# Any free PSUM bank, named in a written order, in place of a ring of six and a ring of two

## The chip, the cores and the metric

The kernel runs on one core of one Trainium2 chip. The metric is the device time of one execution in microseconds (us), as the median of several runs. One further execution was recorded by the hardware profiler; its rows are what the reader sees below. Engines are named as in the profile: PE is the matrix engine, PEld its weight loads, DVE, ACT and POOL the vector, scalar and general engines, SP the engine that issues stores and transposing DMAs.

## The reference, cut to what matters

```python
# q, k, v: (4, 8, 768, 64) float32;  w_in: (512, 2048);  w_out: (2048, 512);  result (3072, 512) float32
scores = q @ k^T / 8 - slope[h] * dist          # per batch and head
keep   = (column < 8) | (0 <= row - column < 96)   # 8 global keys and a window of 96
a      = softmax(where(keep, scores, -1e9))
x      = (a @ v) as (3072 tokens, 512)
out    = relu(x @ w_in) ** 2 @ w_out
```

## The kernel before, in words

The 3072 tokens are 24 tiles of 128 (six a batch), and each two tiles make a block of 256 tokens, 12 blocks in all. Every piece of work is an *op* with a name, made by `Plan.op`. The names that matter here, with the line that the profile shows for their instructions:

- `ld.q.j`, `ld.k.j`, `ld.v.j`, `ld.win.s.c`, `ld.wout.s` (L267): loads of the first tiles and of all weights, one DMA each, issued by POOL. `load.j` (L270), for tiles 6 and up, issues three of them: q, k and v of tile j. All these loads are on one queue and convert float32 to bf16. A ring of eight semaphores makes POOL wait, before each load, for the landing of the eighth load before it.
- `tr`, `T` (L463, L390/L392): transposes of q and k of tiles 0 to 5 on PE, and the copies out of PSUM. From tile 6 on, `T.j` (L487) is one transposing DMA that SP issues. SP issues in its own order, and the instruction waits only for what it reads, for its buffer, and for a semaphore of its own ring.
- `bias`, `sc` (L530, L550): the scores of a tile, in groups of eight matmuls that use half the rows of the PE array each; two PSUM banks a group. `exp` (ACT, L616), `mul` (DVE, L641), `pv` (PE, L703), `norm` (DVE, L733/L734) follow.
- `trx`, `xT` (L771, L390/L392): the attention result transposed, on PE for tiles 0 to 7, later by a transposing DMA (L795).
- `s1.b.s` (PE, L826): step s of eight of the first matrix product of block b, eight matmuls of 128x256 into one bank. `relu` (ACT, L849) and `sq` (ACT L865 or DVE L867) follow.
- `s2.0.s.sub` (PE, L1104): the second product of block 0, with `w_out` as it is. For blocks 1 to 11 the second product is made as seven smaller ones, `s2.b.p1` to `p7`, each in two halves `.0` and `.1` (PE, L975, four matmuls of 128x256 a half). They need sums of the squares (`sum`, DVE) and of the weights (`wsum`, DVE); `p1` and `p2` read `w_out` itself: half `.1` of them reads pieces 4 to 7, the fourth matmul piece 7. `part` and `o` evacuate, `st` (SP) stores.
- `gate.j` (DVE, L436): a tiny write to the buffer that `load.j` fills, so that this load waits for DVE.

No scheduler runs on the chip or in the build. The string `ORDER` lists every op once, in the order in which the program emits them; `@A` and `@V` choose ACT or DVE. Each engine then works through its own instructions in that order, and waits on semaphores for the others.

PSUM has eight banks. Before, they are two pools: `ps_g` with six buffers under one tag, `ps_acc` with two. A new user of a pool gets the buffer after the last one given, round and round, and waits for that buffer's last reader. `ps_acc` holds the first tiles' `pv` and the second product's sums; all else takes turns in `ps_g`:

```python
ps_acc = ctx.enter_context(tc.tile_pool(name="ps_acc", bufs=NACC, space=PSUM))   # NACC = 2
ps_g = ctx.enter_context(tc.tile_pool(name="ps_g", bufs=NG, space=PSUM))         # NG = 6
...
tiles["hT", blk, s] = ps_g.tile([P, 2, 2 * P], FP32, name="hT", tag="g")
...
pool, tag = (ps_g, "g") if last else (ps_acc, "acc")
tiles["acc", blk, bank] = pool.tile([P, HN], FP32, name="acc", tag=tag)
```

Of the kernel before, what the change touches and what calls it, by code (L numbers as in the profile page):

```python
# [59 lines left out]
exp.3.1.0 s1.0.0#2 s1.0.0#3 s1.0.0#4 ld.win.3.0 s1.0.6 norm.2.1 mul.3.0.0 gv.2 ld.k.4 mul.3.1.0 trx.2 mul.3.0.1  # L60
exp.3.1.1 ld.q.4 mul.3.1.1 pv.3.0 pv.3.1 norm.3.0 norm.3.1 relu.0.0 xT.2@A relu.0.6 ld.win.4.0 s1.0.3 s1.0.3#2 gk.3
sq.0.0@A ones.6 trx.3 tr.1.4 T.1.4@A relu.0.3 ld.win.1.0 tr.0.4 xT.3@V sq.0.6@A s1.1.0 T.0.4@V s1.1.6 ld.q.5 ld.k.5
relu.1.0 s1.1.4 sq.0.3@V sq.1.0@V relu.1.6 ld.win.2.1 ld.win.2.0 gv.3 s1.0.1 sq.1.6@V relu.1.4 s1.0.1#2 sc.4.0
sq.1.4@A relu.0.1 tr.0.5 ld.wout.0 exp.4.0.0 s1.1.3 sq.0.1@V sc.4.1 T.0.5@A s1.0.4 mul.4.0.0 exp.4.1.0 ld.win.5.0 E0.1
ld.v.4 s1.0.2 relu.1.3 sq.1.3@A exp.4.1.1 gk.4 s1.1.2 ld.win.7.0 mul.4.1.0 s2.0.0.0 tr.1.5 relu.1.2 s2.0.0.1 exp.4.0.1
s1.0.2#2 s1.0.2#3 sq.1.2@V ld.v.5 T.1.5@A mul.4.0.1 s1.0.2#4 relu.0.4 ld.wout.2 s1.0.5 ld.wout.1 relu.0.2 sq.0.4@V
pv.4.0 s1.1.7 sq.0.2@A mul.4.1.1 norm.4.0 relu.0.5 relu.1.7 pv.4.1 sc.5.0 norm.4.1 sc.5.1 ld.wout.5 exp.5.0.0 sq.0.5@V
s1.1.5 sq.1.7@A gv.4 mul.5.0.0 exp.5.1.0 exp.5.1.1 s1.0.7 exp.5.0.1 ld.wout.3 relu.1.5 mul.5.1.0 trx.4 xT.4@V
mul.5.0.1 s2.0.1.0 mul.5.1.1 pv.5.0 ld.wout.4 norm.5.0 relu.0.7 s1.1.1 ld.wout.7 pv.5.1 norm.5.1 s2.0.1.1 s2.0.2.1
# [5 lines left out]
exp.6.0.0 sq.2.4@V wsum.3.1 s2.1.p5.1 exp.6.1.0 sc.7.0 mul.6.0.0 sc.7.1 s2.1.p7.0 exp.7.0.0 T.8 s2.1.p7.1 gate.9
sq.2.2@A mul.6.1.0 exp.7.1.1 part.1.p7@V s1.2.1 exp.7.1.0 mul.7.0.0 pv.6.0 mul.7.1.1 o.1.p5 exp.7.0.1 norm.6.0 pv.6.1
relu.2.1 mul.7.1.0 mul.7.0.1 s2.1.p4.0 s2.1.p4.1 sq.2.1@A o.1.p4@A s2.1.p3.0 s2.1.p3.1 norm.6.1 load.9 st.1.1 pv.7.1
pv.7.0 o.1.p3 s2.2.p1.0 st.1.0 norm.7.0 trx.6 norm.7.1 s2.2.p1.1 s2.2.p2.0 xT.6@A trx.7 T.9 gk.7 sum.2.0 s2.2.p2.1
xT.7@V sc.8.0 sc.8.1 s1.3.0 s1.3.3 gate.10 sum.2.1 exp.8.0.0 exp.8.1.0 s1.3.7 part.2.p1@A relu.3.0 load.10 exp.8.0.1
gv.7 mul.8.0.0 sum.2.2 sq.3.0@A s1.3.2 exp.8.1.1 mul.8.0.1 s2.2.p6.0 mul.8.1.0 relu.3.7 s2.2.p6.1 relu.3.2 mul.8.1.1  # L80
load.11 sq.3.7@V o.2.p2 pv.8.1 pv.8.0 relu.3.3 s1.3.5 part.2.p6@A norm.8.0 s2.2.p5.0 s2.2.p7.0 sq.3.3@A sq.3.2@A gk.8
sum.2.3 relu.3.5 s2.2.p5.1 sc.9.0 norm.8.1 gv.8 xT.8 exp.9.1.0 mul.9.1.0 sc.9.1 T.10 load.12 sq.3.5@V exp.9.0.0
exp.9.1.1 mul.9.0.0 exp.9.0.1 s2.2.p7.1 s1.3.1 part.2.p7@V mul.9.1.1 s1.3.6 o.2.p5 relu.3.1 relu.3.6 s1.3.4 sq.3.1@A
pv.9.0 mul.9.0.1 s2.2.p4.0 norm.9.0 pv.9.1 norm.9.1 gk.9 s2.2.p4.1 relu.3.4 sq.3.4@A o.2.p4@A s2.2.p3.0 s2.2.p3.1
sq.3.6@A xT.9 s2.3.p1.0 load.13 o.2.p3 s2.3.p1.1 sum.3.0 s2.3.p2.0 part.3.p1@A T.11 sum.3.1 s2.3.p2.1 sum.3.2 sc.10.0
exp.10.1.0 sc.10.1 s2.3.p6.0 s2.3.p6.1 o.3.p2 exp.10.0.0 gv.9 mul.10.1.0 s2.3.p5.0 s2.3.p5.1 part.3.p6@V exp.10.0.1
mul.10.0.0 exp.10.1.1 s2.3.p7.0 mul.10.0.1 load.14 gk.10 mul.10.1.1 s2.3.p7.1 part.3.p7@A pv.10.0 pv.10.1 s1.4.0
norm.10.0 s1.4.7 norm.10.1 relu.4.0 sc.11.0 sc.11.1 s1.4.4 T.12 relu.4.7 s1.4.3 sq.4.0@V exp.11.0.0 o.3.p5 exp.11.1.1
gv.10 mul.11.0.0 exp.11.1.0 s1.4.2 sq.4.7@V exp.11.0.1 load.15 mul.11.1.0 pv.11.0 relu.4.4 mul.11.1.1 mul.11.0.1
relu.4.3 sc.12.0 sq.4.4@A sq.4.3@V s1.4.5 xT.10 st.2.0 relu.4.2 norm.11.0 exp.12.1.0 pv.11.1 s1.4.6 relu.4.5  # L90
exp.12.0.0 s1.4.1 sq.4.2@V mul.12.1.0 sq.4.5@A s2.3.p4.0 norm.11.1 mul.12.0.0 s2.3.p4.1 pv.12.0 xT.11 relu.4.6
relu.4.1 sum.3.3 sq.4.6@A sq.4.1@V T.13 s2.3.p3.0 o.3.p4@A st.2.1 sum.4.0 s2.3.p3.1 o.3.p3 pv.12.1 sum.4.1 sum.4.2
s2.4.p1.0 s2.4.p1.1 s2.4.p2.0 s2.4.p2.1 part.4.p1@A s2.4.p6.0 s2.4.p6.1 part.4.p6@A o.4.p2 s2.4.p5.0 s2.4.p5.1
s2.4.p7.0 s2.4.p7.1 norm.12.0 norm.12.1 load.16 sc.13.0 sc.13.1 s1.5.0 exp.13.1.0 xT.12 T.14 mul.13.1.0 exp.13.1.1
T.15 exp.13.0.0 sum.4.3 s1.5.3 relu.5.0 part.4.p7@A s1.5.5 mul.13.0.0 mul.13.1.1 exp.13.0.1 sq.5.0@V s2.4.p4.0 pv.13.0
s1.5.1 mul.13.0.1 pv.13.1 relu.5.5 sq.5.5@V s1.5.6 relu.5.3 relu.5.1 norm.13.0 norm.13.1 sq.5.1@A xT.13 sq.5.3@V
s1.5.2 s2.4.p4.1 s1.5.4 relu.5.6 o.4.p5 s1.5.7 s2.4.p3.0 s2.4.p3.1 relu.5.2 sq.5.6@A o.4.p4@V st.3.1 gv.13 gk.13
load.18 sq.5.2@V relu.5.4 relu.5.7 sq.5.4@V sc.14.0 sq.5.7@A o.4.p3 sc.14.1 exp.14.0.0 s2.5.p1.0 s2.5.p1.1 s2.5.p2.0
s2.5.p2.1 sum.5.0 exp.14.1.0 st.3.0 T.16 load.17 part.5.p1@A sum.5.1 exp.14.1.1 mul.14.0.0 mul.14.1.0 mul.14.1.1
s2.5.p6.0 s2.5.p6.1 sum.5.2 pv.14.0 exp.14.0.1 s1.6.1 s1.6.0 norm.14.0 part.5.p6@A kl.14 relu.6.0 mul.14.0.1 o.5.p2  # L100
kl.15 relu.6.1 s2.5.p7.0 pv.14.1 s2.5.p7.1 norm.14.1 sq.6.0@A s2.5.p5.0 part.5.p7@A xT.14 sc.15.0 sc.15.1 s2.5.p5.1
s1.6.4 s1.6.3 exp.15.0.0 sum.5.3 exp.15.1.0 s2.5.p4.0 mul.15.0.0 exp.15.0.1 gv.14 sq.6.1@V s1.6.2 s2.5.p4.1 exp.15.1.1
mul.15.0.1 mul.15.1.1 relu.6.3 mul.15.1.0 o.5.p5 st.4.0 load.19 sq.6.3@A relu.6.4 pv.15.0 s2.5.p3.0 norm.15.0 relu.6.2
pv.15.1 o.5.p4@A norm.15.1 sc.16.1 sq.6.2@V sc.16.0 xT.15 s1.6.7 s2.5.p3.1 sq.6.4@A exp.16.1.0 exp.16.0.0 mul.16.1.0
# [1092 lines left out]
```

## Time and profile before

| | us |
|---|---|
| median of 3 runs | 204.45 (204.17 to 205.06) |
| span of the profiled execution, first to last instruction | 202.7 |
| what lies outside the span, median less span | 1.75 |
| PE busy | 196.9 (97%) |
| DVE, ACT, POOL busy | 148.4, 146.1, 75.4 |
| software DMA queue (the loads of POOL), share of 16 engines | 89.0% |

A row of the profile's timeline gives the start and the duration of one or several merged instructions, their engine, line and tiles, and in brackets how long the engine was idle before and what ended that. Matmuls are pipelined: a 128x256 one has a duration of about 270 ns, but the next starts 109 ns later, so work is counted here by the distance of starts. The landing of a DMA is the moment when its semaphore has reached its full count; the profile's DMA view gives the time from issue to landing.

### The profile page before, as it was taken

How to read it: one execution, taken by the hardware profiler on the slowest of the kernel's cores; microseconds unless marked ns; L12 is line 12 of the kernel's file. 1: busy time of each engine (PE TensorE's matmuls, PEld its weight loads, DVE VectorE, ACT ScalarE, POOL GpSimd, SP SyncE). 2: the span in 40 equal slices, each digit the busy share in tenths (PEclk: the TensorE clock that was granted, in tenths of full speed). 3: DMA queues.
4: the chain of work that ended last, by engine and by line, in shares of the span. 5: the costliest groups of instructions: out<-in, count | busy, mean ns of one | idle time of the engine just before them, and what ended most of it. 6: DMA issues, size and time to landing. Idle time of an engine off the chain costs nothing.

```text
span 202.7 us, 5686 instructions
## 1 busy us (share of the span) xinstructions
PE 196.9 (97%) x2272; PEld 166.7 (82%) x2272; DVE 148.4 (73%) x404; ACT 146.1 (72%) x289; POOL 75.4 (37%) x93
## 2 busy tenths in 40 slices
PE   7899999999999999999999999999999999999993
PEld 3668878678889888888988988989988888988883
DVE  8289567882897777885888679679669887717843
ACT  6778899448959865964886987696597677848520
POOL 8999776623339425705059004550130000000000
PEclk9999999999999999999999999999999999999999
DMA  8999999999599999996999956999595323031022
GB/s 126 153 173 179 180 184 205 192 147 182 136 175 139 155 130 121 193 179 91 118 235 137 160 118 145 129 160 204 107 143 105 100 78 29 12 118 55 0 110 102
DMA packets 113965, 27.38 MB, mean 135 GB/s; under 512 B 105490, under 2 KB 111122, under 8 KB 113938
## 3 DMA queue, kind: packets, MB, share of 16 engines
q0 software_dynamic: 80256, 13.37, 89.0%
q1 hardware_dynamic: 33682, 13.64, 33.4%
q8 instruction: 18, 0.29, 0.6%
q14 instruction: 9, 0.07, 0.1%
HBM read 27.26 MB, written 6.29 MB: 166 GB/s over the span
## 4 chain that ended last, share of the span: by engine, by line
PE 88%; POOL 6%; DMA 3%; DVE 0%; issue 0%; POOLq 0%
PE hT L826 41%; PE acc L975 34%; PE sc L550 5%; PE po L703 5%; PE acc L1104 3%; DMA qk<-in_q_dram 3%; POOL qk L267 3%; POOL v L267 2%; POOL win L267 1%; PE tr L463 0%; PE trx L771 0%; DVE o L1051 0%; POOL pbi L327 0%; POOLq L327 0%; POOLq L1178 0%
## 5 line engine op out<-in xcount | busy, mean ns | idle before, releaser
L826 PE MATMUL hT<-xT,win 128*128 128x256 bf16 (+1 forms) x800 | 93.8, 268 | 0.0
L826 PEld LDWEIGHTS <-win 128*128 128x128 bf16 x800 | 74.0, 98 | 9.8
L849 ACT ACTIVATE hr<-hT 128x512 f32<-128x512 f32 x96 | 56.0, 605 | 20.8 <-PE hT L826 17.4
L616 ACT ACTIVATE esc<-sc 128x512 bf16<-128x512 f32 x78 | 42.5, 606 | 5.9 <-PE sc L550 5.3
L270 POOL DMA_DIRECT2D qk<-in_q_dram x18 | 16.2, 902 | 66.9 <-DMA qkT<-qk 51.3
L867 DVE TENSOR_TENSOR hs<-hr 128x512 bf16<-128x512 f32 x43 | 29.5, 685 | 15.7 <-ACT hr L849 15.5
L975 PEld LDWEIGHTS <-hsum 128*128 128x128 bf16 x360 | 33.5, 98 | 5.0 <-issue 0.6
L641 DVE TENSOR_TENSOR at<-esc,E 128x512 bf16<-128x512 bf16 x78 | 30.6, 417 | 6.7 <-ACT esc L616 6.3
L975 PE MATMUL acc<-wsum,hsum 128*128 128x256 bf16 x264 | 34.3, 273 | 0.0
L865 ACT ACTIVATE hs<-hr 128x512 bf16<-128x512 f32 x53 | 33.2, 634 | 0.7
L975 PEld LDWEIGHTS <-hs 128*128 128x128 bf16 x264 | 25.0, 98 | 2.9
L975 PE MATMUL acc<-wout,hs 128*128 128x256 bf16 x176 | 23.0, 273 | 0.0
L1051 DVE TENSOR_TENSOR o<-acc,part 128x256 f32<-128x256 f32 (+2 forms) x34 | 14.0, 411 | 10.7 <-PE acc L975 9.3
L734 DVE TENSOR_TENSOR x<-po,rs 128x256 bf16<-128x256 f32 x48 | 20.4, 424 | 1.7
L390 ACT COPY part<-acc 128x256 f32<-128x256 f32 x24 | 9.0, 374 | 15.0 <-PE acc L975 14.6
L703 PE MATMUL po<-v,at 128*128 128x65 bf16 x352 | 17.8, 194 | 0.4 <-DVE v L751 0.3
L703 PEld LDWEIGHTS <-at 128*128 128x128 bf16 x352 | 15.8, 98 | 2.2 <-issue 0.4
L270 POOL DMA_DIRECT2D v<-in_v_dram x18 | 16.4, 911 | 1.3 <-DMA wout<-in_moe_w_out_dram 1.3
L270 POOL DMA_DIRECT2D qk<-in_k_dram x18 | 16.2, 898 | 0.6 <-DMA wout<-in_moe_w_out_dram 0.6
L932 DVE TENSOR_TENSOR hsum<-hs 128x1024 bf16<-128x1024 bf16 (+1 forms) x24 | 15.4, 641 | 1.3 <-ACT hs L865 1.0
L733 DVE RECIPROCAL rs<-po 128x4 f32<-128x4 f32 x48 | 8.6, 179 | 8.7 <-PE po L703 8.2
L550 PEld LDWEIGHTS <-qkT 64*128 64x128 bf16 x312 | 9.5, 94 | 4.6 <-issue 4.0
(62 smaller groups left out, 182.2 us busy)
## 6 DMA issues: line engine op xcount, KB each, us to landing
out_dram<-o SPq DMA_DIRECT2D x22, 256.0 KB, 2.6
v<-in_v_dram POOLq DMA_DIRECT2D x24, 128.0 KB, 5.6
qk<-in_k_dram POOLq DMA_DIRECT2D x23, 128.0 KB, 5.4
qk<-in_q_dram POOLq DMA_DIRECT2D x23, 128.0 KB, 4.8
wout<-in_moe_w_out_dram POOLq DMA_DIRECT2D x8, 256.0 KB, 9.2
win<-in_moe_w_in_dram POOLq DMA_DIRECT2D x6, 256.0 KB, 7.3
win<-in_moe_w_in_dram POOLq DMA_DIRECT2D x4, 128.0 KB, 6.3
out_dram<-o SPq DMA_DIRECT2D x3, 128.0 KB, 1.7
```

The lines of the kernel that those rows point to most:

```text
L270: nc.gpsimd.dma_start(out=dst, in_=src)
L550: nc.tensor.matmul(out=tiles["sc", j, odd, g][:, at, :], lhsT=left[j - 1][half, pair, :] if kt else qkT[j % NKT][half, 1, pair, :], rhs=qk ...
L616: nc.scalar.activation(out=esc, in_=tiles.pop(("sc", j, odd, g)).rearrange("p a c -> p (a c)"), func=Act.Exp, scale=scale,)
L641: nc.vector.tensor_mul(at, tiles.pop(("esc", j, odd, g)), bias)
L703: nc.tensor.matmul(out=po[:, hi, :], lhsT=tiles["at", j, odd, g][:, at * P : (at + 1) * P], rhs=v_sb[kj][:, h, :], start=(i == 0), stop=(i ...
L734: nc.vector.tensor_tensor(out=x[:, 4 * hf : 4 * hf + 4, :], in0=po[:, :, :D], in1=rs.to_broadcast([P, 4, D]), op=Alu.mult,)
L826: nc.tensor.matmul(out=hT[:, c, cols], lhsT=w_in_sb[s][:, kt, c * P : (c + 1) * P], rhs=tiles["xT", blk][:, kt, cols], start=(kt == 0), st ...
L849: nc.scalar.activation(hr, tiles.pop(("hT", blk, s)), Act.Relu)
L865: nc.scalar.activation(hs, hr, Act.Square)
L867: nc.vector.tensor_mul(hs, hr, hr)
L932: nc.vector.tensor_tensor(out=t[:, i, h], in0=t[:, a, h] if isinstance(a, int) else half_a(blk, *a)[:, h], in1=t[:, b, h] if isinstance(b, ...
L975: nc.tensor.matmul(out=tiles["acc", blk, bank][:, cols], lhsT=left_[:, s], rhs=right_[:, cols], start=first and s == 0, stop=s == NSTEP - ...
```

## The change

All eight banks become eight tiles of their own, made once. A word of `ORDER` can end in a colon and one digit for each bank that the op opens: `sc.7.1:13` takes banks 1 and 3, `s1.2.2:6` takes bank 6. `run` keeps the digits in `o["banks"]`, and `psum(n)` hands the n-th of them to the op. Round-robin is gone; a user still waits for the last reader of its bank. The warm-up matmuls write bank 7. The amount and the kinds of work are the same: the same ops are emitted, with the same shapes. The order of all of them, and the choice of ACT or DVE for some copies and squares, is another. Of the new order these stretches are shown: the loads near the start, `load.6`, `load.7` and `load.8` among the pieces of `w_out`, the first use of pieces 0 to 7, and the end.

```diff
-    def run(self, free=()):
+    def run(self):
...
         for word in ORDER.split():
+            word, _, banks = word.partition(":")
             name, _, letter = word.partition("@")
...
+            o["banks"] = [int(b) for b in banks]
...
-s1.0.2#2 s1.0.2#3 sq.1.2@V ld.v.5 T.1.5@A mul.4.0.1 s1.0.2#4 relu.0.4 ld.wout.2 s1.0.5 ld.wout.1 relu.0.2 sq.0.4@V
...
-s2.0.2.0 s2.0.3.0 sq.1.5@V trx.5 s2.0.4.0 s2.0.5.0 s2.0.3.1 s2.0.4.1 wsum.0.0 relu.1.1 ld.wout.6 load.6 load.7 xT.5@V
...
-s1.2.5 load.8 s2.1.p1.1 sum.1.3 part.1.p1@A s1.2.4 wsum.1.1 relu.2.5 o.0.1@A s2.1.p6.0 relu.2.7 s1.2.2 st.0.1 sq.2.5@A
...
-o.11.p4@V st.11.1#2 s2.11.p3.0 s2.11.p3.1 o.11.p3 st.11.0#2 s2.11.p3.0#2 s2.11.p3.1#2 o.11.p3#2 st.11.0#3
...
+pv.5.0:7 norm.5.0 load.6 load.7 s1.1.5:1 norm.5.1 relu.1.1 s1.1.2:0 ld.wout.0 trx.5:7 ld.wout.2 sq.0.5@V sq.1.1@A
+ld.wout.1 s1.1.4:3 xT.5@V s1.2.0:2 E0.1 relu.1.2 sq.1.2@A s1.2.5:6 s1.2.6:4 T.6 ld.wout.3 relu.0.2 s2.0.0.1:7 relu.2.0
+sq.0.2@V sq.2.0@V relu.2.5 s2.0.0.0:0 T.7 s1.2.7:5 s1.2.4:2 gate.8 relu.1.5 sq.2.5@V s2.0.1.0 s1.2.3:6 sq.1.5@V
+ld.wout.4 relu.1.4 sq.1.4@V sum.1.0 s2.0.2.0 s2.0.1.1 s2.0.2.1 relu.2.7 load.8 T.8 sq.2.7@V sc.7.1:13 wsum.2.0
+relu.2.6 relu.2.4 wsum.0.0 sum.1.2 sc.7.0:54 sq.2.6@A sum.1.1 relu.2.3 ld.wout.5 sc.6.0:26 gk.7 sq.2.4@V exp.7.1.1
+ld.wout.6 exp.6.0.0 exp.7.0.1 sum.1.3 s2.0.3.1 s2.0.3.0 ld.wout.7 mul.7.1.1 s2.1.p2.0:3 mul.6.0.0 exp.6.1.0 s2.0.4.1
+s2.0.4.0 mul.7.0.1 s2.1.p1.0:2 wsum.1.0 exp.7.1.0 s2.0.5.0 s2.0.5.1 mul.6.1.0 pv.6.0:1 gate.9 exp.7.0.0 mul.7.1.0
+s1.2.2:6 pv.6.1:4 mul.7.0.0 norm.6.0 s2.0.6.0 norm.6.1 wsum.0.1 s2.1.p1.1 relu.2.2 pv.7.0:5 sq.2.3@A load.9 trx.6:1
...
+st.11.1#2 s2.11.p3.0 s2.11.p3.1 o.11.p3 st.11.0#2 s2.11.p3.0#2 s2.11.p3.1#2 o.11.p3#2 sum.10.3 part.10.p1@A s2.10.p6.0
+s2.10.p6.1 s2.10.p2.0:5 s2.10.p2.1 part.10.p6@A s2.10.p7.0 s2.10.p7.1 o.10.p2 s2.10.p5.0 s2.10.p5.1 part.10.p7@V
+s2.10.p4.0 s2.10.p4.1 o.10.p5 st.11.0#3 s2.10.p3.0 o.10.p4@A st.10.1 s2.10.p3.1 o.10.p3 st.10.0
...
-    NG = 8 - NACC
-    G = ("g", NG)
+    NBANK = 8
+    G = ("bank", NBANK)
...
-    ps_acc = ctx.enter_context(tc.tile_pool(name="ps_acc", bufs=NACC, space=PSUM))
-    ps_g = ctx.enter_context(tc.tile_pool(name="ps_g", bufs=NG, space=PSUM))
+    ps = ctx.enter_context(tc.tile_pool(name="ps", bufs=1, space=PSUM))
...
+    banks = [ps.tile([P, 4 * P], FP32, name=f"bank_{i}", tag=f"bank_{i}") for i in range(NBANK)]
+    given = []
+
+    def psum(n=0, dt=FP32):
+        b = banks[given[n]]
+        return b if dt == FP32 else b.bitcast(dt)[:, : 4 * P]
...
-                tiles["hT", blk, s] = ps_g.tile([P, 2, 2 * P], FP32, name="hT", tag="g")
+                tiles["hT", blk, s] = psum().rearrange("p (a c) -> p a c", a=2)
...
-                            pool, tag = (ps_g, "g") if last else (ps_acc, "acc")
-                            tiles["acc", blk, bank] = pool.tile([P, HN], FP32, name="acc", tag=tag)
+                            tiles["acc", blk, bank] = psum()[:, :HN]
...
-    for o in plan.run({"PE": 4.2, "DVE": 4.2, "ACT": 5.3, "DMAQ": issue[1]}):
-        if o["emit"]:
-            o["emit"](o["engine"])
+    for o in plan.run():
+        given[:] = o["banks"]
+        o["emit"](o["engine"])
```

The other users (`tr`, `sc`, `pv`, `trx`, block 0's `acc`) change in the same way.

More of the change, by code (lines that the diff above doesn't have):

```diff
@@ L60 @@
[L60 to L69, printed above, removed]
@@ L75 @@
[L75 to L84, printed above, removed]
@@ L85 @@
[L85 to L104, printed above, removed]
@@ new lines @@
+s1.2.2:6 pv.6.1:4 mul.7.0.0 norm.6.0 s2.0.6.0 norm.6.1 wsum.0.1 s2.1.p1.1 relu.2.2 pv.7.0:5 sq.2.3@A load.9 trx.6:1
+part.1.p1@A wsum.1.1 s2.0.6.1 s2.1.p6.0 s2.0.7.0 wsum.3.1 s2.1.p6.1 norm.7.0 pv.7.1:6 wsum.2.1 s2.0.7.1 part.1.p6@A
+o.0.0@A s2.1.p7.0 o.0.1@V sq.2.2@A xT.6@A s2.1.p2.1 T.9 wsum.3.0 s2.1.p7.1 o.1.p2 s1.2.1:4 part.1.p7@A s2.1.p4.0
+relu.2.1 norm.7.1 load.11 trx.7:5 s2.1.p5.0 sc.8.1:07 xT.7@V gate.10 exp.8.1.1 sc.8.0:16 exp.8.1.0 exp.8.0.0 gv.7
+s2.1.p5.1 s2.1.p4.1 sq.2.1@V s2.2.p1.0:4 o.1.p5 sum.2.0 s2.1.p3.0 s2.1.p3.1 gk.8 mul.8.1.0 mul.8.0.0 o.1.p4@A
@@ L329 @@
     nc.scalar.activation(junk, zero[:, :1], Act.Exp)
-    warm = ps_g.tile([P, 4 * P], FP32, name="warm", tag="g")
     for i in range(NWARM):
-        nc.tensor.matmul(out=warm, lhsT=zero[:, :P], rhs=zero, start=True, stop=True)
+        nc.tensor.matmul(out=banks[7], lhsT=zero[:, :P], rhs=zero, start=True, stop=True)
     nc.vector.scalar_tensor_tensor(
@@ L718 @@
                 key=base + 2 + 2 * hf,
-                takes=("acc", NACC, [users]) if j < 2 else (*G, [users]),
+                takes=(*G, [users]),
             )
@@ L995, in seven @@
                         key=base + 1.0 + i * 8 / 7 + 0.5 * g,
-                        takes=((*G, [users[bank]]) if last else ("acc", NACC, [users[bank]])) if i < 2 and g == 0 else None,
+                        takes=(*G, [users[bank]]) if i < 2 and g == 0 else None,
                     )
@@ L1099, in emit_s2 @@
                 if s == 0:
-                    pool, tag = (ps_g, "g") if own else (ps_acc, "acc")
-                    tiles["acc", blk, sub, half] = pool.tile([P, w], FP32, name="acc", tag=tag)
+                    tiles["acc", blk, sub, half] = psum()[:, :w]
                 hs = tiles["hs", blk][:, s]
@@ L1117 @@
                 key=8 * blk + s + 2.0 + (0 if not last else 8 * sub + 8 * (half or 0)),
-                takes=((*G, [users]) if own else ("acc", NACC, [users])) if s == 0 else None,
+                takes=(*G, [users]) if s == 0 else None,
             )
```

132 lines of the change are left out of this document (82 added, 50 removed).

## The prediction

> **What bounds the kernel now.** The page first: who is busy, and whether the clock holds.
>
> ```profile
> PE 196.9 (97%) x2272; PEld 166.7 (82%) x2272; DVE 148.4 (73%) x404; ACT 146.1 (72%) x289; POOL 75.4 (37%) x93
> PEclk9999999999999999999999999999999999999999
> DMA  8999999999599999996999956999595323031022
> ```
>
> PE is the bound, at full clock, and the DMA engines are full for the first quarter. How much of PE's time is idle is read from distances of starts: a 128x256 matmul starts 0.109 us after the last, four 128x128 take 0.22, a group of eight score matmuls 0.226, eight of `pv` 0.236 (0.118 where a tile has four). Entering a run of score groups costs 0.096 more and leaving it 0.12 (around 60 us: 59.76, where the last `s2` matmul should end its turn, to 59.85; 60.28 to 60.40), so 0.216 a run. By these prices all work is 185.1 us; the written order has 26 such runs, 5.6 us, in all 190.75. From 33 us to 198.9 us the starts leave no other gap above 0.06 us: no wait for a PSUM bank, which is what free banks could take away. What PE loses lies at the start and at the end. The chain of waits around 20 us (start, us, what):
>
> ```profile
> 13.97 6.52 DMA qk<-in_q_dram
> 20.49 0.05 issue
> 20.54 0.40 PE tr L463 x4
> 20.93 3.51 PE hT L826 x40
> ```
>
> and PE's timeline around 31 us:
>
> ```profile
> 30.85 0.41 PE L703 MATMUL po<-v,at 128*128 128x65 bf16 x8
> 31.20 1.05 PE L826 MATMUL hT<-xT,win 128*128 128x256 bf16 x8
> ```
>
> PE goes by landings: `q` of tile 4 at 20.49, and at 31.20 `s1.1.7`, whose piece 7 of `w_in` landed at 31.16. Ahead of it lies 23.09 us of PE work, so PE runs 31.20 - 23.09 = 8.11 us behind its own work. I call this the lag: the largest of (landing, less PE work ahead of its first use) over all loads. After that it never grows by waiting until the last product:
>
> ```profile
> 198.39 0.82 PE L975 MATMUL acc<-wout,hsum 128*128 128x192 bf16 x8
> 198.59 0.42 DVE L392 COPY o<-acc 128x256 f32<-128x256 f32 x1
> 199.25 0.36 DVE L1051 TENSOR_TENSOR o<-acc,part 128x192 f32<-128x192 f32 x1 [0.24 <-PE acc L975]
> 199.66 0.39 PE L975 MATMUL acc<-wout,hsum 128*128 128x64 bf16 x8 [0.45 <-DVE o L1051]
> 200.09 0.22 DVE L1051 TENSOR_TENSOR o<-acc,part 128x64 f32<-128x64 f32 x1 [0.48 <-PE acc L975]
> ```
>
> The sum for before: lag 8.11 + work 190.75 + 0.61 (the wait before the last eight) + 0.41 (small gaps) = 199.88, where PE's last matmul is issued; then 0.20 to the add, 0.22, 0.03 to the store, 1.45 to its landing and 0.91 to the end: 202.7, the span. The median is 204.45, 1.75 above the span.
>
> **Part by part.** *Work* is the same: 185.1 us. *Score runs*: 22 in the new order, as the groups of a tile stand together more often: 4 x 0.216 = -0.86.
>
> *The end.* Block 11's products now come before block 10's, whose squares are long done: the 0.61 wait goes. What is late next is the store: the last op is a 128x256 add (0.42 by its row, for 0.22) and a store of 256 KB instead of 32 KB; the late stores of that size landed 2.0 to 2.6 after issue. 0.20 + 0.42 + 0.03 + 2.2 + 0.91 = 3.76 for 2.81: +0.95. Both: +0.34.
>
> *The loads.* This decides. POOL's queue now holds `load.6` and `load.7` ahead of all eight pieces of `w_out`, and `load.8` ahead of the last three; before, they came behind. The timeline of POOL before, at the seam:
>
> ```profile
> 31.45 0.70 POOL L267 DMA_DIRECT2D wout<-in_moe_w_out_dram  x1 [0.66 <-DMA win<-in_moe_w_in_dram]
> 32.28 0.90 POOL L270 DMA_DIRECT2D qk<-in_q_dram  x1
> ```
>
> and what the view of line L267 says of its loads:
>
> ```profile
> DMA to landing us min/median/max: 4.4/7.1/9.6
> ```
>
> The last piece of `w_out`, issued at 31.45, landed at 40.97, and the next tile's q, k and v at 41.82, 42.65 and 43.48: 2.51 us a tile. The queue is served in order and is full, so three tiles ahead put the last piece at 40.97 + 7.5 = 48.5.
>
> Then the transposes. `T.6` and `T.7` wait only for their tile's q and k (SP has nothing else in front), so they now run at 32 to 41 us, while `w_out` is still on its way, and `T.8` before the last pieces. Before, all of them ran after `w_out`. What a transposing DMA costs the loads beside it, from both sides: the three loads that landed while the first one (issued 42.73) was under way took 2.65 instead of 2.51, so 0.14; the loads of v by the DMA view (median us from issue to landing), first in the stretch 124 to 134 us, with two transposes, then in 54 to 58 us, without:
>
> ```profile
> v<-in_v_dram POOLq DMA_DIRECT2D x2, 128.0 KB, 7.5
> ```
>
> ```profile
> v<-in_v_dram POOLq DMA_DIRECT2D x1, 128.0 KB, 4.6
> ```
>
> 2.9 for two, 1.45 each. I take 1.1, nearer the upper row, since there too a queue of loads stood behind: 3.3 for three, bounds 0.4 and 4.4. The last piece lands at 51.8.
>
> The Trainium skill ("DMA: Bandwidth & Descriptors", Queues, rings and completion order) says that each DMA engine takes turns, packet by packet, between the queue rows that have work; the stretch from 124 us agrees (7.5 for 4.6), the first transpose hardly. With that page's 261 GB/s for a transposing DMA (Latency and other measured facts), an estimate for its 256 KB is 1.0 us each, 3.0 for three, which would make the sum 0.3 less.
>
> Who needs the last piece: the fourth matmul of `s2.1.p1.1`. Ahead of it stand, in the new order, 3.05 us of `tr`, 2.18 `bias`, 3.16 `sc`, 2.83 `pv`, 1.31 `trx`, 20.06 `s1`, 6.54 `s2`, seven score runs (1.51) and three matmuls (0.33): 40.97. The lag becomes 51.8 - 40.97 = 10.8. A second path gives about the same: `wsum.2.0` holds DVE until piece 3 lands (40.9 + 2 x 1.1 = 43.1), and behind it, up to the `mul` that `pv.6.0` needs, stand three `wsum` (0.69), three `sum` (0.64), `gk` 0.27, `sq` 0.69, four `mul` (0.42): 6.6, less at most 0.9 of overlap; PE has 39.1 ahead of `pv.6.0`, so a lag of 9.7 to 10.6. The first loads alone would give 8.3 (piece 1 of `w_in` at 20.3, 11.95 of work ahead). Lag: +2.7.
>
> *The banks.* A bank behind an ACT reader comes free 0.8 us after its last matmul was issued (0.16 of matmul tail, 0.605 by the `relu` row) if ACT is idle. In mid-kernel the new order asks for such banks after as little as 1.10 us of PE work (`s2.3.p1`, `s2.5.p1`, `s1.4.6`), the old one after 1.34; ACT is 72% busy. Two more links are short: `gk.10` between `sc.10` and `sc.11` (1.96 us, before never under 5 in mid-kernel) and `xT.23` before `s1.11.0` (4.36; norm 0.6, transpose 2.4 to 3.7). Nothing in the trace shows such waits: between 0 and 2.5; I take 0.3, nearer to the tightest cases of before, which cost nothing.
>
> Sum: 2.7 - 0.86 + 0.34 + 0.3 = +2.5. Span 205.2, time 206.9 (span plus 1.75, rounded).
>
> **Rivals.**
> - *The transposes cost the loads next to nothing* (for: the first one of before; against: 124 to 134 us). The last piece lands at 48.5 to 48.9, lag 7.5 to 7.9, so the first loads decide with 8.3: 0.2 - 0.86 + 0.34 + 0.3 = 0.0: 204.4. Chance 0.18.
> - *Faster*: besides, the landings come earlier. Before, one half piece of `w_in` (L267, landed 15.40) took 1.70 us where others took 0.65 to 0.78; in the new order other loads stand around those halves. If that 0.9 is not lost again, the lag is 7.4, and with no bank waits the change is -0.7 - 0.86 + 0.34 = -1.2: 203.2. It needs transposes under 0.2 us each. Chance 0.09.
> - *Banks come late*: some fifteen reclaims at 1.1 to 1.25 us have 0.3 to 0.45 to spare; where ACT's queue ahead of the reader is longer, PE waits, 0.15 on average would be 2.3. With the lag: 208.9. For: ACT's load; against: no such wait before at 1.34. Chance 0.14.
> - *The clock falls* while PE waits for `w_out`. Before, the first matmuls ran at half pace (0.426 us for 128x512, against 0.216 later) for 3.1 us, so a fall costs some 1.5: 208.4. Against: with 2.5 us of gaps between 10 and 20 us the granted clock stayed at 1.0. Chance 0.05. The Trainium skill ("TensorE: Matmul & The Clock Gate", Part 1) puts the fall after an idle window of about 3.4 us; no gap that I expect is so long.
>
> **How the numbers follow.** The forecast has 0.52, 0.02 is left for what I don't see. About 0.5% (1.0 us) is what a measurement here can tell from no change: slower by more has 0.52 + 0.14 + 0.05 + 0.02 = 0.73, the same 0.18, faster 0.09. The forecast's own range, from transposes at 0.7 to 1.45 and bank waits up to 1, is 205.4 to 208.5. With most of the first rival below and the bank waits above: 204.0 to 209.4; the faster case and some tails, about 0.18, lie outside.
>
> **What would show it.** PE waiting for `wout` at L1112 and at L984 between 37 and 52 us, above all before `s2.1.p1.1`, and `w_out` landing until about 52; DVE's `wsum` held by it; `T.6` issued near 32 us. No gaps in PE after 55 us but the score runs, 22 in all. A last add of 128x256 and a store that lands some 2.2 us after its issue. I am wrong if PE never waits for `w_out`, or if gaps after 55 us sum to over 1 us.

## The result, and the profile after

The changed kernel takes 212.62 us (median of four, 211.68 to 214.13) where the kernel before, run beside it, takes 204.75 (204.17 to 205.57): 1.039 times as long, 95% interval 1.036 to 1.0425. The forecast was 206.9, at most 209.4. The profiled execution took 214.13 us with a span of 212.4, 9.7 us over the span of before. Slow executions are left out of the times below: two of the four of `e4_half_packets` (213.32 and 214.5 us) and the profiled one of `e2_small_first` (218.15 us), of which only the first 60 us are read.

The page of the changed kernel: busy time of PE, and in 40 slices the granted clock and the share of the DMA engines.

```profile
PE 199.1 (94%) x2269; PEld 167.8 (79%) x2272; DVE 151.6 (71%) x410; ACT 146.2 (69%) x283; POOL 75.4 (36%) x93
...
PEclk9999999995999999999999999999999999999999
DMA  9999999999999959999999998969591432104022
```

The one "5" in the clock row is new, and it marks where most of the time went. Up to 42 us PE loses what it lost before (its lag there is 8.3 us, for 8.1). Then, in PE's timeline (start, duration, in brackets how long PE was idle before and what ended that):

```profile
41.84 1.46 PE L1112 MATMUL bank<-wout,hs 128*128 128x512 bf16 x6
47.93 0.29 PE L561 MATMUL bank<-qkT 64*128 64x128 bf16 x2 [4.63 <-DMA qkT<-qk]
```

L561 is `sc.7.1`, the first scores of tile 7. By starts PE stands still for 4.8 us, until the transposing DMA `T.7` has landed. `T.6` was issued at 32.49 and landed at 45.01, `T.7` at 35.02 and 47.89. The view of the tile `qkT` shows how far that is from the rest, first for the changed kernel, then for the kernel before:

```profile
DMA to landing us min/median/max: 3.1/5.3/12.9
```

```profile
DMA to landing us min/median/max: 3.0/4.6/7.9
```

The windows of two microseconds show what follows (from:to, length of the window, busy us and instructions of PE, PEld, DVE, ACT, POOL, then granted clock, DMA share, GB/s; the DMA share adds up the times of packets that overlap, so it can be over 1):

```profile
44.00:46.00 2.00, 0.00 (x0) 0.00 (x0) 1.65 (x3) 0.00 (x0) 0.00 (x0) 1.00 1.96 120
46.00:48.00 2.00, 0.07 (x2) 0.07 (x4) 0.00 (x0) 0.00 (x0) 0.00 (x0) 0.75 2.75 147
48.00:50.00 2.00, 1.94 (x25) 1.41 (x27) 1.09 (x3) 1.17 (x3) 0.00 (x0) 0.50 1.39 201
50.00:52.00 2.00, 1.84 (x7) 1.05 (x7) 2.00 (x6) 1.81 (x5) 0.00 (x0) 0.50 1.24 206
52.00:54.00 2.00, 2.00 (x8) 0.83 (x7) 0.90 (x4) 0.28 (x1) 1.46 (x2) 0.54 0.66 134
```

While PE waits, its clock is halved (at 47.02 in the trace's clock records, for 6.83 us), and from 47.93 to 53.85 every matmul starts at twice its distance: 5.92 / 2 = 2.96 us lost. The window 52 to 54 holds 8 matmuls and counts as fully busy, so the busy share alone would not tell. Two more waits come later, for a transposing DMA each (PE's timeline):

```profile
84.93 1.03 PE L836 MATMUL bank<-xT,win 128*128 128x256 bf16 x8 [0.92 <-DMA xT<-x]
...
101.68 0.23 PE L561 MATMUL bank<-qkT 64*128 64x128 bf16 x2 [0.78 <-DMA qkT<-qk]
```

The end (timeline of SP's queue and DVE): a full add, and the store of 256 KB issued at 209.45 that landed at 211.46.

```profile
208.45 1.33 SPq L1082 DMA_DIRECT2D out_dram<-o  x2
209.00 0.42 DVE L1060 TENSOR_TENSOR o<-bank,part 128x256 f32<-128x256 f32 x1 [1.39 <-PE bank L984]
```

The sum against before: the lag at `sc.7.1` is 47.93 - 34.81 = 13.1 us in place of 8.1 (+5.0), the half clock +2.96, the two later waits 1.08 and 0.95 by starts (+2.0), four score runs fewer -0.86, the end +0.9 (3.74 us from the start of the last matmul to the end of the span, for 2.86). That is 10.0; 9.7 was measured, and the rest of -0.3 was not followed. The other three executions were 1.2 to 2.5 us shorter: the mean granted clock of the four is 0.984, 0.990, 0.984 and 0.992, and since 6.83 us at half clock lower the mean over 212 us by 0.016 and 3.41 us by 0.008, the clock was halved for about 6.8 us in two of the four and, by this estimate, for about 3.4 us in the other two.

### The profile page after: what moved, and what is told of

Same layout as the page of the kernel before. It is cut to its first block, busy times and chain, and to the rows that moved or that the text cites. A ratio compares the mean times of both kernels' runs of the same rounds, so it can differ in the third digit from the quotient of the medians.

```text
span 212.4 us, 5687 instructions
## 1 busy us (share of the span) xinstructions
PE 199.1 (94%) x2269; PEld 167.8 (79%) x2272; DVE 151.6 (71%) x410; ACT 146.2 (69%) x283; POOL 75.4 (36%) x93
## 4 chain that ended last, share of the span: by engine, by line
PE 50%; DMA 4%; DVE 0%; SPq 0%; issue 0%; DVEq 0%
PE bank L984 23%; PE bank L836 22%; DMA qkT<-qk 4%; PE bank L561 2%; PE bank L713 2%; DVE o L1060 0%; SPq L805 0%; SPq L499 0%; DVEq L1060 0%
## 5 line engine op out<-in xcount | busy, mean ns | idle before, releaser
L836 PE MATMUL bank<-xT,win 128*128 128x256 bf16 (+1 forms) x800 | 95.5, 268 | 1.1 <-DMA xT<-x 0.9
L859 ACT ACTIVATE hr<-bank 128x512 f32<-128x512 f32 x96 | 57.0, 599 | 30.5 <-PE bank L836 27.1
L627 ACT ACTIVATE esc<-bank 128x512 bf16<-128x512 f32 x78 | 43.0, 605 | 11.9 <-PE bank L561 10.6
L877 DVE TENSOR_TENSOR hs<-hr 128x512 bf16<-128x512 f32 x41 | 28.0, 688 | 14.1 <-ACT hr L859 13.8
L984 PE MATMUL bank<-wsum,hsum 128*128 128x256 bf16 x264 | 36.0, 273 | 0.0
L984 PE MATMUL bank<-wout,hs 128*128 128x256 bf16 x176 | 24.9, 277 | 0.0
L744 DVE TENSOR_TENSOR x<-bank,rs 128x256 bf16<-128x256 f32 x48 | 20.4, 425 | 1.7
L561 PE MATMUL bank<-qkT 64*128 64x128 bf16 x192 | 13.3, 226 | 6.0 <-DMA qkT<-qk 5.4
L561 PEld LDWEIGHTS <-qkT 64*128 64x128 bf16 x312 | 10.0, 98 | 10.6 <-DMA qkT<-qk 6.2
L713 PE MATMUL bank<-v,at 128*128 128x65 bf16 x352 | 17.8, 193 | 0.3 <-DVE v L761 0.2
L1060 DVE TENSOR_TENSOR o<-bank,part 128x256 f32<-128x256 f32 (+2 forms) x34 | 14.0, 411 | 5.5 <-PE bank L984 4.3
L743 DVE RECIPROCAL rs<-bank 128x4 f32<-128x4 f32 x48 | 8.6, 180 | 8.5 <-PE bank L713 8.2
```

What stands on the lines that cost most here:

```text
L561: nc.tensor.matmul(out=tiles["sc", j, odd, g][:, at, :], lhsT=left[j - 1][half, pair, :] if kt else qkT[j % NKT][half, 1, pair, :], rhs=qk ...
L627: nc.scalar.activation(out=esc, in_=tiles.pop(("sc", j, odd, g)).rearrange("p a c -> p (a c)"), func=Act.Exp, scale=scale,)
L713: nc.tensor.matmul(out=po[:, hi, :], lhsT=tiles["at", j, odd, g][:, at * P : (at + 1) * P], rhs=v_sb[kj][:, h, :], start=(i == 0), stop=(i ...
L744: nc.vector.tensor_tensor(out=x[:, 4 * hf : 4 * hf + 4, :], in0=po[:, :, :D], in1=rs.to_broadcast([P, 4, D]), op=Alu.mult,)
L836: nc.tensor.matmul(out=hT[:, c, cols], lhsT=w_in_sb[s][:, kt, c * P : (c + 1) * P], rhs=tiles["xT", blk][:, kt, cols], start=(kt == 0), st ...
L859: nc.scalar.activation(hr, tiles.pop(("hT", blk, s)), Act.Relu)
```

## The experiments

*Theory T*: the new order puts the transposes of tiles 6 and 7 beside the `w_out` transfers, PE asks for them too early, and its clock falls in the wait. *Rival M*: naming banks costs by itself, or (*M'*) the loss is spread over the whole new order. *Rival W*, my forecast's own step: the late `w_out` pieces set the end. Ratios are to the kernel before, run on the same chip, 204.6 to 204.7 us each time. Every kernel has named banks; where an order is changed, the banks are named anew for it if need be. Words that don't matter are left out of the diffs at "...", and in experiment 3 those of other engines too.

**1. The mechanism alone.** `ORDER` of before; each opening op names the bank that the rings gave it.

```diff
-tr.0.0 T.0.0@A ld.k.1 tr.1.0 ld.q.1 tr.1.1 ...      (rings of six and two)
+tr.0.0:0 T.0.0@A ld.k.1 tr.1.0:1 ld.q.1 tr.1.1:2 ... (the same banks by name)
```

> The order of before, and every user of PSUM names its bank; the names are those that the ring of six and the ring of two gave in before, so that only the way of claiming is changed. Theory T (the order put the transposes of tiles 6 and 7 beside the w_out transfers; PE waits 5 us for them, and its clock falls after it): as before, 204.2 to 205.2 us, the transposes of tiles 6 and 7 issued after the last w_out piece and landed in 4 to 5.5 us. Rival M (naming banks itself costs, for example by waits that a ring does not make): at least 2 us over before, with waits for banks spread over the span. Rival W (my forecast's own step: the late w_out pieces) says here what T says.

Measured: 204.75 us, ratio 1.0002 (0.9987 to 1.0018). Naming the banks costs and brings nothing that the interval (0.3 us either way) can tell; all of the loss comes with the new order, its choice of banks and engines included.

**2. Where in the order.** Up to `s2.2.p6.1` (55 us of PE work) the new order, then all that is left in the order of before.

```diff
-ORDER = new
+ORDER = new[up to 55 us of PE work] + [op for op in old if not yet written]
```

> The reverse: the changed kernel's order up to 55 us of PE work, and from there the order of before. Theory T: the gap of 5 us before the scores of tile 7 and the fall of the clock are there as in the changed kernel; the last store is the small one again and no transpose is issued close to its scores later: 209.5 to 212 us. Rival M': about half of the loss, 207 to 209 us.

Measured: 211.87 us, ratio 1.033 (1.0295 to 1.037). The first 55 us of work bring 7.3 of the 7.9 us. Its PE timeline has the same wait:

```profile
49.42 0.29 PE L561 MATMUL bank<-qkT 64*128 64x128 bf16 x2 [5.76 <-DMA qkT<-qk]
```

**3. PE asks later.** Only words of PE's queue (and what ACT and DVE do for them) move.

```diff
-s2.0.2.1 sc.7.1:13 sc.7.0:54 sc.6.0:26 s2.0.3.1 s2.0.3.0 ... s2.0.4.1 s2.0.4.0 ... s1.2.2:6
+s2.0.2.1 s2.0.3.1 s2.0.3.0 s1.2.2:2 s2.0.4.1 s2.0.4.0 sc.7.1:13 sc.7.0:54 sc.6.0:26
```

> The changed kernel with 2.6 us of PE work that needs nothing of tiles 6 and 7 (the products of block 0 with w_out pieces 3 and 4, and s1.2.2) moved in front of the scores of tiles 7 and 6. No transfer is moved. Theory T (the order asks for the transpose of tile 7 earlier than the DMA engines, which carry the w_out pieces beside it, deliver it): the wait before the scores falls from 4.8 to about 2.2 us, too short for the clock to fall; what is left at 53 us is the wait for the last w_out pieces (52.7 us, needed at 41.0 us of work: 11.7 us of lag in place of 13.1): 208.5 to 210.5 us. Rival (the wait is the same for whoever comes first, because PE is held by something else at 43 to 48 us, such as the operations on DVE and ACT): 211.5 to 214 us.

Measured: 209.37 us, ratio 1.022 (1.019 to 1.024). The DMAs landed as in the changed kernel (`T.7` at 47.63), and the wait shrank by what was put ahead of it:

```profile
47.67 0.23 PE L561 MATMUL bank<-qkT 64*128 64x128 bf16 x2 [1.95 <-DMA qkT<-qk]
```

The clock held in this execution (1.00 in every window; two of the other three have a mean of 0.99). 2.6 us of moved work brought 3.2 us, so the wait is for this DMA and not for PE's neighbours.

**4. The transposes taken away.** q and k of tiles 6 and 7 are transposed by PE, with copies on ACT and DVE.

```diff
-    JQK, JX = 6, 8
+    JQK, JX = 8, 8
-... T.6 ... T.7 ...
+... tr.0.6:7 tr.1.6:0 T.0.6@A T.1.6@V ... tr.0.7:1 T.0.7@A tr.1.7:3 T.1.7@V ...
```

> The changed kernel with q and k of tiles 6 and 7 transposed by PE through PSUM (as tiles 0 to 5 are: 4 x 0.218 us of PE work and four copies on ACT and DVE) and not by DMA. The suspected transfers are taken away, the order of all loads and of the scores stays. Theory T: no gap before the scores of tile 7; the last w_out piece lands 2.5 to 3.3 us earlier, at 49.4 to 50.2 us, just in time for its product: no gap over 1 us and no fall of the clock from 40 to 60 us; 204.5 + 0.9 + 0.95 - 0.4 and up to 2 us of later waits: 205.9 to 208 us. Rival W (the place of the w_out pieces behind the loads of tiles 6 and 7 decides): 208.5 to 211 us, with the waits at the products that read the w_out pieces.

Measured: 209.74 us, ratio 1.024 (1.019 to 1.029): 2.9 us better than the changed kernel, with 0.9 us more work on PE, but 1.7 us over the upper end of what Theory T gave. The time lies in the range of Rival W (208.5 to 211 us), but Rival W's sign is missing: PE waits for no piece of `w_out`. The wait for the DMA is gone; two waits for banks stand in its place, since ACT evacuates them late (PE's timeline):

```profile
46.18 0.21 PE L562 MATMUL bank<-qkT 64*128 64x128 bf16 x1 [0.66 <-ACT hr L860]
47.33 0.38 PE L562 MATMUL bank<-qkT 64*128 64x128 bf16 x7 [0.93 <-ACT hr L860]
```

The `w_out` pieces ahead of `load.8` came 1.28 us apart in place of 1.6 to 2.6, the last of them at 42.89; but the last piece of all still landed at 52.26: POOL stood before `load.8` until 41.10 for `gate.8`, which DVE now reached later, and from 41.5 to 42.5 us the queue moved only 23 packets. Behind the wait that was removed stood the next ones.

**5. Only the loads put back.** All `w_out` pieces ahead of the loads of tiles 6 to 8, as before; PE's order stays.

```diff
-load.6 load.7 ... ld.wout.0 ... ld.wout.2 ... ld.wout.4 ... load.8 ... ld.wout.7
+ld.wout.0 ld.wout.2 ld.wout.1 ld.wout.3 ld.wout.4 ld.wout.5 ld.wout.6 ld.wout.7 load.6 load.7 ... load.8
```

> The changed kernel with only the order of the loads put back: all w_out pieces ahead of the loads of tiles 6, 7 and 8, so that the transposes meet no w_out piece. PE's order is the changed kernel's. Theory T: the transposes are quick again (4 to 5.5 us each) but start later, the second lands at 50.6 us as in before, while the scores stand at 34.8 us of work: a gap of 7 to 8 us before them, the clock falls after it, and no wait for w_out: 214.5 to 217.5 us, slower than the changed kernel. Rival W (the w_out pieces behind the loads of tiles 6 and 7 are the cost): 204.5 to 207 us.

Measured: 216.87 us, ratio 1.057 (1.053 to 1.061).

```profile
51.42 0.29 PE L561 MATMUL bank<-qkT 64*128 64x128 bf16 x2 [8.23 <-DMA qkT<-qk]
```

Here `w_out` was in by 40.98, and it is the slowest of the three orders of loads that were run with this PE order. Rival W falls: the scores, and not the `w_out` products, are what PE asks for too early. (The transposes took 7.6 and 6.1 us, not 4 to 5.5, although no piece of `w_out` ran beside them; the last section says where that time lies.)

**6. The clock alone.** Matmuls of zeros in the wait.

```diff
             if j >= NBIAS:
                 open_sc(gs)
+            for i in range(16 if j == 7 and gs[0] == 1 else 0):
+                nc.tensor.matmul(out=banks[given[0]], lhsT=zero[:, :P], rhs=zero, start=True, stop=True)
```

> The changed kernel, and in front of the scores of tile 7 PE runs 16 extra products of 128x512 zeros into the bank that these scores are about to take (16 x 0.216 us = 3.5 us, inside the wait for the transpose of tile 7). No transfer is moved. Theory T: the wait stays (its end is still at about 48 us), but no gap is longer than about 1.7 us, the granted clock stays at full after it, and the 2.9 us of matmuls at half pace are gone: 208.8 to 210.5 us in place of 212.6. Rival: the half pace after the gap has another cause than the gap (what PE does then is slow in itself): 212 to 213 us, with the starts at twice the distance from 48 to 54 us as in the changed kernel.

Measured: 211.29 us, ratio 1.032 (1.029 to 1.035); the profiled execution 209.94. The two windows that were at 0.50 in the changed kernel:

```profile
48.00:50.00 2.00, 2.00 (x32) 1.39 (x33) 1.43 (x4) 1.57 (x3) 0.00 (x0) 1.00 1.42 201
50.00:52.00 2.00, 2.00 (x14) 1.12 (x13) 2.00 (x7) 1.58 (x3) 0.00 (x0) 1.00 1.24 206
```

The scores start at 47.96 as before the edit, and no clock falls (mean 0.997 to 1.000 in all five executions): the half pace came from standing still. The medians differ by 1.3 us, less than the 2.1 I had as the least; the mean clocks above suggest why: in two of the changed kernel's four executions the fall lasted only one half as long as in the profiled one.

**7. How the two queues share.** The first four `w_out` pieces in two DMAs of 256 columns.

```diff
-    w_out_sb[s] <- moe_w_out[f, :]          one DMA, packets of 1024 bytes
+    w_out_sb[s][:, :, m] <- moe_w_out[f, m]  two DMAs, packets of 512 bytes, for s < 4
```

> The changed kernel with each of the w_out pieces 0 to 3 loaded by two DMAs of 256 columns (packets of 512 bytes) in place of one of 512 columns (1024 bytes). Order and bytes are the same. Theory T in its closer form (hardware queue and software queue take turns packet by packet): beside packets of half the size a transpose moves 1.6 times as many packets per us (one pair of packets takes 2.5 + 1.2 in place of 5.1 + 1.2 ns: 270 per us against 160), so the transpose of tile 6 lands in 6 to 8 us instead of 12.5 and that of tile 7 at 42 to 44.5 us instead of 47.9; the gap before the scores of tile 7 falls below 2 us, no fall of the clock: 206 to 209 us. Rival (they share by bytes, or the transpose is slow by itself while any load runs): it lands at 45 and 48 us as before the edit, 212 to 214 us.

Measured: 209.21 and 211.73 us, ratio 1.027 (1.019 to 1.035), the widest interval here. The ratio rests on two executions 2.5 us apart, so here the time decides little and the trace has to. The DMA view of the stretch 37 to 41 us (packets, MB, share of the 16 engines), first the changed kernel, in which `T.6` (hardware queue) and `w_out` (software queue) run side by side:

```profile
q0 software_dynamic: 643, 0.62, 91.6%
q1 hardware_dynamic: 641, 0.16, 30.3%
```

then the kernel with half packets:

```profile
q0 software_dynamic: 832, 0.40, 92.7%
q1 hardware_dynamic: 826, 0.20, 55.7%
```

Packet for packet in both: beside packets of 1024 and of 512 bytes the two queues take turns. The Trainium skill ("DMA: Bandwidth & Descriptors", Queues, rings and completion order) says that each DMA engine goes round the queues that have work, packet by packet, and the counts of the two queues here agree to 0.7%. So a transpose of 1024 packets of 256 bytes goes at the pace of the big packets beside it, 160 per us, where `w_out` alone moved 842 packets in 4 us (before, 33 to 37 us). Beside the 128-byte packets of tile 8's loads the counts are not equal; in experiment 8, from 37.5 to 38.5 us:

```profile
q1 hardware_dynamic: 453, 0.12, 108.2%
q0 software_dynamic: 120, 0.02, 25.1%
```

Whether the software queue was short of work there, no run shows. Half packets gave 206 per us and not 270; `T.6` landed in 9.8 us instead of 12.5, `T.7` still at 47.12. PE waited only 0.35 us for it, because it had waited 2.2 us for `w_out` piece 1 first. The turns hold beside these packets; my price for a pair of packets, 3.7 ns, was too low (4.85).

**8. Small packets first.** `load.8` (with `gate.8`) ahead of `w_out`, so that the transposes would meet small packets.

```diff
-load.6 load.7 s1.1.5:1 ... ld.wout.0 ... ld.wout.4 ... load.8 T.8
+load.6 load.7 load.8 s1.1.5:1 ... ld.wout.0 ... ld.wout.4 ... T.8
```

> The changed kernel with the loads of tile 8 (three of small packets) issued directly behind those of tile 7, ahead of all w_out pieces, and the DVE operation that they wait for moved up with them. PE's order is the changed kernel's. The transposes of tiles 6 and 7 now meet small packets for most of their time. Theory T: they land in about 6 us each instead of 12.5 and 12.9, by about 39 and 42 us; the 5 us gap before the scores of tile 7 is under 1 us; the granted clock does not fall at 48 us (2.9 us back); what is left is the wait for the last w_out pieces, which still land at about 52 us: 206 to 209 us. Rival W (the w_out pieces alone set the end): since the last of them lands no earlier than before this edit, no gain, 211.5 to 214 us. Rival M: no gain either.

Measured: 213.57 us, ratio 1.041 (1.037 to 1.045). A miss. `T.6` landed at 43.20, `T.7` at 51.09, and the first `w_out` piece at 44.29, for which PE now waited:

```profile
44.33 0.59 PE L1112 MATMUL bank<-wout,hs 128*128 128x512 bf16 x1 [6.09 <-DMA wout<-in_moe_w_out_dram]
```

I had forgotten that the new order wants the first `w_out` piece at 38 us. And the transposes met the small packets only for some 2 us: the first packet of `T.6` moved at 36.26, 3.5 us after its issue, and from 38.5 us on the `w_out` pieces ran. They took 10.5 and 15.8 us, not 6. In none of the three orders of loads that were run (the changed kernel's, this one, experiment 5's) did the engines bring tiles 6 to 8, two transposes and `w_out` by the time at which this order of PE asks for them.

**9. Is this place all?** The order of before up to `o.2.p5` (62 us of PE work), then the new one; and the same with the cut at 52 us, ahead of `s1.3.0`.

```diff
-ORDER = new
+ORDER = old[up to 62, or 52, us of PE work] + [op for op in new if not yet written]
```

> The order of before up to 62 us of PE work, and from there the changed kernel's order for all that is left; banks are named for it. Theory T (the loss lies between 40 and 60 us, at the transfers of tiles 6 to 9): no gap over 1 us before 62 us of work, then only what the changed order brings later: 204.7 + 0.95 for the last store - 0.2 for a score run fewer, and 0.5 to 2.5 us of waits for transposes, which the changed order issues 0.1 to 4 us of PE work ahead of their scores where before has 5 to 13: 205.5 to 208 us. Rival M' (the loss is spread over the new order): 209 us or more.

> The order of before up to 52 us of PE work, and from there the changed kernel's order. The scores of tiles 6 to 8 stand as in before, those of tile 9 at 53.4 us of work in place of 59.3. Theory T in its wider form (the changed order asks for every tile's transpose earlier than its loads can bring it; tile 7 was only the first): the transpose of tile 9 lands at 63 us, its scores are due at 61.6: a wait of 1.5 to 3 us there, and 1.2 to 3.2 us more than before from what comes later: 207 to 210 us, 1.5 us or more over the same kernel with the cut at 62. Theory T in its narrow form (only the transposes of tiles 6 and 7 beside the w_out pieces): the same as with the cut at 62, 205.5 to 208 us.

Measured: 209.95 us, ratio 1.025 (1.021 to 1.029), and 217.53 us, ratio 1.062 (1.057 to 1.0675). The first lies where Rival M' put it (209 us or more). Both went against Theory T in its narrow form, and the wider one had the sizes too small. With the cut at 62, PE's timeline:

```profile
74.62 0.23 PE L561 MATMUL bank<-qkT 64*128 64x128 bf16 x2 [1.83 <-DMA qkT<-qk]
```

and the clock fell for 3.41 us behind it. With the cut at 52, the chain of waits (start, us, what):

```profile
55.01 4.33 DMA qk<-in_k_dram
...
59.39 8.30 DMA qkT<-qk
...
67.74 0.62 PE bank L561 x5
```

`T.9` took 8.3 us and the scores of tile 9 waited 3.9. PE also waited 2.1 us for DVE at 62.59 and 2.1 us for an `xT` at 88.56, and the clock fell twice, for 6.83 and 3.41 us. The changed kernel has neither the wait for tile 9 nor, with the cut at 62, the one for tile 10, at the same words of its order: it comes there with a lag of 13 to 16 us in place of 8, and the transposes have had that much more time. The losses don't add: the first part alone costs 7.3, the rest alone 5.4, both together 7.9. What is wrong with the new order is not in one place: in these runs it made PE wait for the transposes of, among others, tiles 7 and 14 (changed kernel), 9 and 10 (here) and 12 (0.33 us in experiment 3). Of the 18 tiles with a transposing DMA it writes the scores of 12 nearer to that DMA than before, among them tile 7 (4.4 us of PE work between them for 7.1), 9 (6.9 for 8.2), 10 (2.5 for 7.2) and 14 (5.1 for 8.4). But this distance alone does not tell who waits: tile 12 has 3.4 for 2.1, and tile 22, with 0.1 for 14.1, made PE wait in none of the profiles. That the first place that waits pays for the others is argued from the sums; no run moves them all.

**10. Put right by hand.** Both halves of the place as before (loads of experiment 5, and 7.4 us of products ahead of the scores of tiles 7 and 6), the rest of the new order kept.

```diff
-... s2.0.2.1 sc.7.1:13 sc.7.0:54 sc.6.0:26 s2.0.3.1 ...
+... s2.0.2.1 s2.0.3.1 ... s2.0.7.1 s2.1.p2.1 s2.1.p6.0 sc.7.1:14 sc.7.0:56 sc.6.0:70 ...
```

> The changed kernel with both halves of the disputed place put back in the manner of before, all the rest as changed: all w_out pieces are issued ahead of the loads of tiles 6, 7 and 8, and the products of blocks 0 and 1 (7.4 us of PE work) stand in front of the scores of tiles 7 and 6. Banks are named for the new order. Theory T: the w_out pieces land by 41 to 42 us, the transposes of tiles 6 and 7 at 47 and 50.6 us, where the scores stand at 42.2 us of work, so the lag stays at 8 to 9 us, no gap over 1 us and no fall of the clock between 40 and 60 us: 205.3 to 207.5 us (204.5 + 0.7 + 0.95 for the last store - 0.4 for two score runs fewer, and up to 2 us of waits for transposes at 84 and 101 us). Rival M' (the loss is spread over the new order, not in this place): 210 to 213 us.

Measured: 216.38 us, ratio 1.056 (1.053 to 1.059), 9 us over what I expected, and over Rival M' too. The wait for `T.7` was 0.84 us, as intended; PE then waited 1.43 us for a bank at 53.93, and the next scores of the unchanged remainder paid:

```profile
67.15 0.29 PE L561 MATMUL bank<-qkT 64*128 64x128 bf16 x2 [3.59 <-DMA qkT<-qk]
```

That is tile 9, whose loads wait for `T.6` to free their buffer and for `gate.9`; its transpose landed at 67.10. The clock fell at 66.07, in this wait, for 6.83 us.

**11. Two small edits on the order of before.** One score run fewer, and PE not held by DVE before its last matmuls.

```diff
-sc.6.0 part.1.p6@A s2.1.p5.0 ... sc.7.0 mul.6.0.0 sc.7.1
+part.1.p6@A s2.1.p5.0 sc.6.0 sc.7.0 sc.7.1
-s2.11.p3.0 s2.11.p3.1 o.11.p3 st.11.0#2 s2.11.p3.0#2 s2.11.p3.1#2 o.11.p3#2 st.11.0#3
+s2.11.p3.0 s2.11.p3.1 s2.11.p3.0#2 s2.11.p3.1#2 o.11.p3 st.11.0#2 o.11.p3#2 st.11.0#3
```

> The order of before with named banks and two small edits that they allow: the scores of tiles 6 and 7 in one run of three (six banks at once, as in the changed kernel), and the last 64 columns of block 11's final product in front of the operation on DVE that reads the other 192, so that PE doesn't wait 0.61 us for it. By the prediction's own prices: a score run fewer is 0.22 us, the wait 0.61 us less the 0.22 us by which that operation now starts later: 204.7 - 0.2 - 0.3 = 204.2 us, ratio 0.9965 to 0.999. Rival (both lie beside other work): 204.6 to 204.8 us.

Measured: 205.31 us, ratio 1.0034 (1.0009 to 1.006): slower. The 0.61 us wait is gone, but from the start of `s2.11.p3.0` to the issue of the last store it is now 2.23 us for 1.95, since the two adds follow each other on DVE. And PE waited elsewhere:

```profile
81.79 0.23 PE L561 MATMUL bank<-qkT 64*128 64x128 bf16 x2 [1.09 <-DMA qkT<-qk]
```

`T.11` took 7.6 us here and 4.8 in before, where it landed 1.7 us ahead of its scores. Which of the edits, or the banks named anew, made it slow was not tried. No version that beats the kernel before was found.

## Why the prediction was wrong

- *What bounds the kernel, and the sign*: right. PE is the bound, the place is the loads at 31 to 53 us, and the change is slower. That the loads decide, by the lag (landing less work ahead), held; but not by the load that was named. Both signs of being wrong that the prediction gave came: PE waits for `wout` nowhere in the changed kernel, and the gaps after 55 us sum to 2.0 us.
- *The loads of `w_out`*: the landing came as forecast, the last piece at 52.67 (51.8 forecast), and `T.6` was issued at 32.49 (32). The price of 1.1 us a transpose is not confirmed by that, and part of the agreement is luck. Without the transposes of tiles 6 and 7 (experiment 4) the fifth piece came 5.1 us after the first, for 7.6 in the changed kernel, so `T.6` and part of `T.7` cost 2.4; but the last piece still landed at 52.26, because POOL was held longer before `load.8`. And `T.8`, the third that I priced, was issued only at 48.36.
- *The step that failed* is "`T.6` and `T.7` ... now run at 32 to 41 us". I priced what a transpose costs the loads and not what the loads cost the transpose: 12.5 and 12.9 us from issue to landing in place of 4.4 and 5.1, so that `T.7` landed at 47.89 and not at 41. Only a part of that is the pace beside `w_out` (at most 3.9 of the 8.1 us more for `T.6`, last section); `T.7` stood behind `T.6` until 43.07. I asked for the lag only of the op that reads the last piece of `w_out` (40.97 us of work ahead, 10.8 forecast, 11.7 by its landing), and never of `sc.7.1`, which has 34.81 ahead: 47.93 - 34.81 = 13.1. Experiment 3 shows it by moving the op, experiment 4 by taking the transposes away, experiment 5 by taking the late `w_out` pieces away without gain.
- *The clock*: the rival came true on top of the forecast (chance 0.05), though in the wait for `T.7` and not for `w_out`. My reason against it, that 2.5 us of gaps before had left the clock alone, was about shorter gaps than 4.8. Its price was 1.5; 2.96 was measured in the profiled execution, about 1.7 in two others by their mean clock.
- *The banks*: 0.3 forecast, nothing seen in the changed kernel after 55 us. Experiment 4 shows why this is no verdict on them: with the DMA wait gone, banks cost 2 us at 46 us.
- *Score runs*: 22, and -0.86 fits the sum. *The end*: the longer store came nearly as forecast (+0.9 for +0.95), but the 0.61 us wait did not go; it ends at 203.25, before block 10's last products.
- *No gaps after 55 us*: wrong by 2.0 us, the short way from `T.14` and `xT` to their readers. I had compared such distances for banks, and for `gk` and one `xT`, but not for `T`.

## What to carry to other kernels

A DMA that is issued earlier is not landed earlier: price what the transfers beside it do to it, and for every load ask who needs it first, with the work ahead of that reader. A hand-written order hides its slips behind the largest lag, so putting right the first wait may make the next one larger (experiments 9 and 10); compare each transfer's landing with its reader's place over the whole order, and not only at the place that changes. When the matrix engine has to wait, keep it busy: 16 matmuls of zeros in the gap were worth 1.3 us.
